# Attention from last tile to first, with WO work, QKV weights and the last x statistics in other slots (sliding dilated attention beside a ReLU feed-forward block, one core)

## The chip, the cores and the metric

The kernel runs on one core of a Trainium2 chip. The metric is the device time of one execution in microseconds (us). Five engines work side by side, each through its own instruction stream in order: TensorE (PE, matmuls; PEld is its weight load), VectorE (DVE), ScalarE (ACT), GpSimd (POOL) and SyncE (SP). SP issues most of the DMA transfers; POOL issues the transfers that add results to the output.

## The reference

`x` has 2048 tokens of 576 features, `wqkv` is 576 x 1728, `wo` 576 x 576, `w1` 576 x 4608, `w2` 4608 x 576, all float32.

```python
xn = _layernorm(x)                              # eps 1e-5, no gain, no bias
qkv = xn @ wqkv                                 # 32 heads of Dh = 18
idx = pos[:, None] - np.arange(8)[None, :] * 2  # W = 8 keys: this token and 7 before it, in steps of 2
logits = einsum("bhsd,bhswd->bhsw", q, kg) * Dh ** -0.5   # idx < 0 masked with -1e9
o = einsum("bhsw,bhswd->bhsd", softmax(logits), vg)
out = x + o.reshape(B, S, D) @ wo + maximum(xn @ w1, 0) @ w2
```

## The kernel before

**Two phases.** The step between keys is 2, so even and odd tokens never meet in the attention. The kernel therefore runs in two phases, `ph` 0 (even tokens) and 1 (odd). Each phase has 1024 tokens in eight tiles `i` of 128. Partition p holds the tokens 16p to 16p + 15 of the sequence, so the tiles of a phase are eight consecutive tokens of each partition. The key window of tile i, `window(k, i)`, is rows i to i + 7 of a block of 15 rows: rows 0 to 6 are the *halo*, a copy of the last seven key rows of the partition before (`halos`, four DMAs `att<-att`, L533), and rows 7 to 14 are the partition's own tiles. Value rows are laid out in the same way.

**Precision.** All products are made of float32 values split into a high and a low part: `two` copies the high part on ACT (L172) and subtracts for the low part on DVE (L176) or POOL (L174). Every weight goes through it before PE reads it.

**The feed-forward block** gives PE most of its work. The first six blocks of 128 hidden features per phase run in 24 *slots* (`BASE` 0 and 1000; `h_mm`, `h_two`, `o_mm`, `o_two`). The other 30 run in Strassen-like *groups* `g` of eight steps (`prologue` for group 0, then `group`), in pairs, whose `w1` blocks are loaded by `sw_load` (L895, L900), mixed on POOL (`sw_mix`) and split (`sw_prep`). `w2` blocks are loaded by L207. Matmuls on the two halves of the array, into different banks, run in pairs (L163; L142 for paired lists).

**QKV and attention.** The 32 heads are four units `u` of eight. QKV of unit 0 is computed in slots, of units 1 to 3 in groups 5, 11 and 17. After a unit's QKV its halos are copied, and `attention` puts its DVE work as a list of items into the queue `bg`: a multiply and a sum per tile for the logits (L563, L566), a mask on POOL (L569) after one of the sums, softmax, then a multiply and adds per tile for the values, and at the end a transpose and eight writes to DRAM (`o_out`, L618, L622). `run_bg(margin)` takes items off that queue while a planned DVE time stays within `margin` of a planned PE time; the plan (`t["pe"]`, `t["dve"]`) is made when the program is built. Buffers `pr` are used by turns, one at a time.

**WO.** When the last unit is written out, WO weights (`wo_load`, L257, L260) are split (`wo_split`, on ACT and DVE) and the attention rows come back (`ot_in`). `ot_plan` lists this work with delays, in us of the planned PE time, to the entry that it depends on: ("wl", 6 + ...) is that long after the WO loads. `wo_block(ph, r)` multiplies four tiles' rows by WO; `evict` copies PSUM to an `ev` tile (L711) and POOL adds it to the output. The blocks of phase 0 run in `seam`, between the phases, and in the first slots of phase 1, those of phase 1 in `epilogue`.

**x of phase 1** passes in phase 0 through `xq_load` (L404), `stats` (L303 to L307), `xq_norm` (L409), `turn` (L382) and `blocks_out` (L391), in the buffers of the attention tile that are free then.

**Order.** The kernel's order is written out by hand: each engine gets its instructions in the order of emission. `at(n, f)` emits f in slot n between the two halves of PE work (hidden features, then outputs), `late(n, f)` after the second. `on(ph, g, i, "T" or "O", f)` emits f in step i of group g, after the first or the second part of the step. A DMA's buffer and data dependences become semaphore waits of the instruction that needs them.

Of the kernel before, what the change touches and what calls it, by code (L numbers as in the profile page):

```python
# [19 lines left out]
P = 128  # L20
# [50 lines left out]
def tile_body(ctx: ExitStack, tc: tile.TileContext, x, wqkv, wo, w1, w2, out):  # L71
# [416 lines left out]
    def qkv_half(ph, u, tb, second, new):  # L488

        a = att(ph).rearrange("p (r c) -> p r c", c=UD)  # L490
        q0, v0 = Q_ROW[u % 2], V_ROW[u % 2]
        if tb == 0 and not second:
            assert len(bg) <= 26, (ph, u, len(bg))
            QO[ph, u] = a[:, q0 : q0 + NI]
            KK[ph, u] = a[:, K_ROW : K_ROW + W - 1 + NI]
            VV[ph, u] = a[:, v0 : v0 + W - 1 + NI]
        wq = WQ[ph, u]
        xt = XT[ph, tb]

        def run(h, terms):  # L500
            return [
                (PQ[h], xt[:, a, h * P : (h + 1) * P], wq[:, b, :], not second and j == 0, second and j == len(terms) - 1, 3 * UD)
                for j, (a, b) in enumerate(terms)
            ]

        if not second:
            if new:
                z = ps_o.tile([P, 2, 512], F32, name="po")
            for h in range(2):
                if new:  # L510
                    PQ[h] = z[:, h, 0 : 3 * UD]
                else:
                    PQ[h] = ps_m.tile([P, 3 * UD], F32, name="pm")
            PQ[2] = mm_rows((run(0, LOWER_MORE), run(1, UPPER_MORE)))
            return
        mm_rows((run(1, LOWER), run(0, UPPER)), PQ[2])
        for h in range(2):
            j, pq = 2 * tb + h, PQ.pop(h)
            step = K_ROW + W - 1 - q0
            nc.scalar.activation(  # L520
                a[:, q0 + j : q0 + j + 2 * step + 1 : step, :], pq.rearrange("p (s c) -> p s c", s=3), AF.Copy
            )
# [19 lines left out]
    def attention(ph, u):  # L542
# [15 lines left out]
        def qk_mul(i):  # L558
            if i % 2 == 0:
                both = prp.tile([P, 2, W, UD], F32, name="pr")  # L560
                pr[i], pr[i + 1] = both[:, 0], both[:, 1]
            q = qo[:, i, None, :].to_broadcast([P, W, UD])
            nc.vector.tensor_tensor(pr[i], q, window(k, i), op=ALU.mult)  # L563

        def qk_sum(i):
            nc.vector.tensor_reduce(lg[:, i], pr.pop(i).rearrange(heads, d=Dh), axis=AX.X, op=ALU.add)  # L566
            if i == NI - 2:
# [63 lines left out]
        for i in range(0, NI, 2):  # L631
            for f in (qk_mul, qk_sum):
                for j in (i, i + 1):
# [404 lines left out]
    def plan_strassen(ph):  # L1038
# [20 lines left out]
        for u in range(1, NU):  # L1059
# [9 lines left out]
            on(ph, g + 2, 2, "O", attention, ph, u)  # L1069
# [22 lines left out]
    def ot_plan(ph):  # L1092
# [4 lines left out]
        for kt in range(2, KT + 1):  # L1097
            z.append((("ws", kt), wo_split, (ph, kt), None, (("wl", 6 + 1.4 * (kt - 2)),)))
        for r in range(4):
            z.append((("in", r), ot_in, (ph, r), free if r == 3 else done, ((("in", r - 1), 5.0),) if r else (("wl", 5.0),)))  # L1100
# [33 lines left out]
    def prologue(ph, n0):  # L1134
# [24 lines left out]
        run_bg(1.0)  # L1159
# [75 lines left out]
    def wo_block(ph, r, parts=(0, 1, 2, 3)):  # L1235
        ot_go(ph, r)
        for k in parts:
            wo_half(ph, r, k % 2, k > 1)

# [104 lines left out]

    todo_late = {}
# [6 lines left out]
    for ph in range(NPH):  # L1352
# [15 lines left out]
        if ph == 0:  # L1368
# [4 lines left out]
            for i in range(NI):  # L1373
# [3 lines left out]
                late(n + 1 + odd, do)  # L1377
                if i < 6:
                    late(n + 2 + odd, xq_norm, i)
                    late(n + 2 + odd, turn, xq(i), 1, i)  # L1380
                    at(n + 4, blocks_out, xq(i), 1, i)
                else:
                    on(0, 0, 2 + 3 * odd, "O", xq_norm, i)
                    on(0, 0, 2 + 3 * odd, "O", turn, xq(i), 1, i)
                    on(0, 0, 7 + odd, "O", blocks_out, xq(i), 1, i)
                at(13 + i, nc.sync.dma_start, o_v[1, i], x_v[1, i])
        else:
# [3 lines left out]
            for r in range(1, NTB):  # L1391
                at(b + 3 * r, wo_block, 0, r)
            at(b + 10, wq_load, ph, 0)
# [5 lines left out]
        late(b + UNIT0[ph] + NI + 1, attention, ph, 0)  # L1399
# [118 lines left out]
    for ph in range(NPH):  # L1518
        b = BASE[ph]
        for n in range(b + (FIRST if ph == 0 else 0), b + NOLD - 2):  # L1520
            g = n - n % 2 + LAG
            if n < ROW0:
# [12 lines left out]
            run_bg(margin(n))  # L1535
# [31 lines left out]
```

## Time and profile before

| | us |
|---|---|
| median of 3 runs | 1171.43 |
| their range | 1170.77 to 1171.69 |
| the profiled execution | 1176.77 |
| its span in the trace | 1175.0 |
| PE busy in it | 1125.7 (96%) |
| DVE busy | 816.7 (70%) |
| ACT busy | 562.2 (48%) |
| POOL busy | 472.7 (40%) |

The profile shows one execution. The busy time of an engine is the time in which it has an instruction under way. A row of the timeline gives start, duration, engine, line and operation, the tiles (out<-in), and in square brackets how long the engine had stood idle before and what ended the wait. A row of the waits view gives the engine, tile and line that waited, what it waited for, the total in us, how often, and the longest. The granted clock is the share of full TensorE speed that the chip allowed; over the whole execution it is 0.984. Line numbers are those of the kernel before; in the changed kernel lines after L630 stand 3 lower, those of the end some more.

### The profile page before, as it was taken

Reading aid. Unit: us, or ns where it says so; the run is one execution under the profiler, and the core shown is the slowest. Engines: PE = TensorE matmul, PEld = TensorE weight load, DVE = VectorE, ACT = ScalarE, POOL = GpSimd, SP = SyncE. Lnnn points to the kernel's source line nnn. Section 1 sums busy time; section 2 is a strip of 40 time slices with the busy share of each in tenths; the row PEclk is TensorE's granted clock in tenths of the full one; section 3 lists DMA queues with packets and bytes.
Section 4 is the critical chain, followed back from the end, with each engine's and each line's share of the span. In section 5 each row is a group of like instructions: output and inputs, shape, how many; then the busy total and the mean of one; then the engine's idle time right before and its main releaser. Section 6 shows DMA issues by size and latency. Waiting matters only on the chain.

```text
span 1175.0 us, 38355 instructions
## 1 busy us (share of the span) xinstructions
PE 1125.7 (96%) x16410; PEld 1103.4 (94%) x16410; DVE 816.7 (70%) x1249; ACT 562.2 (48%) x1316; POOL 472.7 (40%) x514
## 2 busy tenths in 40 slices
PE   8999899999999999999997999999999999999996
PEld 8998899999999999998997999999999999999895
DVE  7675788698798788874315438877896886888431
ACT  4443463454355455556534235635644634555540
POOL 2323452353354355553323135434524523555331
PEclk9999899999999999999999999999999999999898
DMA  7479795786697598899947157858858957888984
GB/s 217 156 170 197 139 196 91 142 173 118 141 184 129 98 185 140 156 184 281 189 63 157 24 106 169 157 86 174 173 95 160 204 92 164 143 155 155 215 131 111
DMA packets 159810, 176.82 MB, mean 150 GB/s; under 512 B 36232, under 2 KB 107144, under 8 KB 159608
## 3 DMA queue, kind: packets, MB, share of 16 engines
q0 software_dynamic: 44352, 81.45, 47.5%
q1 hardware_dynamic: 114604, 92.03, 26.8%
q8 instruction: 129, 2.11, 0.7%
q10 hardware_dynamic: 684, 0.88, 0.2%
q14 instruction: 41, 0.34, 0.1%
HBM read 74.07 MB, written 95.70 MB: 144 GB/s over the span
## 4 chain that ended last, share of the span: by engine, by line
PE 73%; DMA 12%; DVE 6%; issue 3%; ACT 3%; SPq 2%; POOL 1%; DVEq 0%; ACTq 0%; POOLq 0%
PE po L163 23%; PE po L142 19%; PE ph L163 12%; PE pm L163 10%; PE pm L142 5%; DMA st<-in_w 4%; DMA out<-ev 3%; PE ph L142 3%; DVE ar L176 2%; DMA att<-od 1%; DMA att<-att 1%; ACT ev L711 1%; DMA xS<-od 1%; DMA od<-pr 1%; DVE ar L757 1%
## 5 line engine op out<-in xcount | busy, mean ns | idle before, releaser
L163 PE MATMUL po<-ar 64*128 64x320 f32 (+1 forms) x5760 | 475.6, 292 | 7.0 <-DVE ar L176 6.3
L163 PEld LDWEIGHTS po<-ar 64*128 64x128 f32 x5760 | 414.9, 186 | 11.3 <-DVE ar L176 9.0
L724 POOL DMA_DIRECT2D out<-ev x256 | 226.6, 1026 | 399.3 <-ACT ev L711 373.0
L163 PE MATMUL ph<-xT,ar 64*128 64x256 f32 x2520 | 328.7, 279 | 15.6 <-ACT pm L975 7.5
L163 PEld LDWEIGHTS ph<-xT,ar 64*128 64x128 f32 x2520 | 291.8, 187 | 21.9 <-ACT pm L975 12.3
L711 ACT ACTIVATE ev<-po 128x512 f32<-128x512 f32 (+1 forms) x268 | 172.8, 650 | 218.2 <-PE po L163 110.4
L163 PE MATMUL pm<-xS,ar 64*128 64x256 f32 x2160 | 267.9, 279 | 1.8 <-ACT u L979 0.7
L163 PEld LDWEIGHTS pm<-xS,ar 64*128 64x128 f32 x2160 | 242.3, 187 | 3.7 <-DVE ar L757 1.1
L176 DVE TENSOR_TENSOR ar<-st,ar 128x256 fp32r<-128x256 f32 (+3 forms) x232 | 146.1, 641 | 64.2 <-ACT ar L172 54.3
L172 ACT ACTIVATE ar<-st 128x256 fp32r<-128x256 f32 (+3 forms) x304 | 147.9, 500 | 21.5 <-DMA st<-in_w 16.2
L174 POOL TENSOR_TENSOR ar<-st,ar 128x256 fp32r<-128x256 f32 (+1 forms) x72 | 94.3, 1323 | 158.6 <-ACT ar L172 156.7
L907 POOL TENSOR_TENSOR st<-st 128x256 f32<-128x256 f32 x120 | 135.9, 1145 | 12.1 <-DMA st<-in_w 7.8
L142 PE MATMUL po<-wq,xT 64*128 64x432 f32 x1296 | 136.4, 353 | 0.0
L142 PEld LDWEIGHTS po<-wq,xT 64*128 64x128 f32 x1296 | 123.6, 184 | 1.5
L163 PE MATMUL ph<-xS,ar 64*128 64x256 f32 x720 | 103.2, 276 | 1.0 <-ACT ph L975 0.8
L563 DVE TENSOR_TENSOR pr<-att 128x1152 f32<-128x1152 f32 x64 | 89.3, 1399 | 18.4 <-DMA att<-att 18.2
L598 DVE TENSOR_TENSOR pr<-att 128x1152 f32<-128x1152 f32 x64 | 89.9, 1423 | 12.2 <-ACT att L520 11.9
L163 PEld LDWEIGHTS ph<-xS,ar 64*128 64x128 f32 x720 | 94.0, 184 | 2.6 <-ACT ph L975 2.0
L566 DVE TENSOR_REDUCE att<-pr 128x64 f32<-128x1152 f32 x64 | 84.9, 1338 | 0.0
L142 PE MATMUL po<-ar 64*128 64x256 f32 (+1 forms) x984 | 73.1, 293 | 2.7 <-ACT ev L711 2.7
L757 DVE SCALAR_TENSOR_TENSOR ar<-u,ar 128x256 fp32r<-128x256 f32 x60 | 31.7, 528 | 63.2 <-ACT ar L753 63.1
L605 DVE TENSOR_TENSOR pr<-pr 128x1152 f32<-128x1152 f32 x64 | 71.5, 1117 | 1.4
(120 smaller groups left out, 1356.4 us busy)
## 6 DMA issues: line engine op xcount, KB each, us to landing
out<-ev POOLq DMA_DIRECT2D x268, 288.0 KB, 6.2
st<-in_w SPq DMA_DIRECT2D x72, 288.0 KB
st<-in_w SPq DMA_DIRECT2D x120, 128.0 KB
att<-att SPq DMA_DIRECT2D x16, 441.0 KB
att<-in_wqkv SPq DMA_DIRECT2D x28, 216.0 KB
od<-pr SPq DMA_DIRECT2D x32, 128.0 KB
att<-in_x SPq DMA_DIRECT2D x14, 288.0 KB
st<-in_w SPq DMA_DIRECT2D x60, 64.0 KB
```

Of the source, the lines that this page charges most:

```text
L142: ins = nc.tensor.matmul(o, l[z], r[z], start=start, stop=stop)
L163: b.ins = nc.tensor.matmul(b.ap, l[part], r[part], start=start, stop=stop, skip_group_check=skip)
L172: nc.scalar.activation(hi, src, AF.Copy)
L174: nc.gpsimd.tensor_tensor(lo, src, f32(hi), op=ALU.subtract)
L176: nc.vector.tensor_tensor(lo, src, f32(hi), op=ALU.subtract)
L563: nc.vector.tensor_tensor(pr[i], q, window(k, i), op=ALU.mult)
L566: nc.vector.tensor_reduce(lg[:, i], pr.pop(i).rearrange(heads, d=Dh), axis=AX.X, op=ALU.add)
L598: nc.vector.tensor_tensor(pr[i].rearrange(heads, d=Dh), e, window(v, i).rearrange(heads, d=Dh), op=ALU.mult)
L605: nc.vector.tensor_tensor(o, z[:, :, 0:n], z[:, :, n : 2 * n], op=ALU.add)
L711: nc.scalar.activation(acc[:, :, cols], z[:, :, 0 : cols.stop - cols.start], AF.Copy)
L724: ADDED[ph, 2 * tb + k] = nc.gpsimd.dma_start(o_v[ph, 2 * tb + k], acc[:, k, :], accum_op=ALU.add)
L907: nc.gpsimd.tensor_tensor(stg(o), stg(a), stg(b), op=op)
```

## The change

Six things are changed in the order of emission; no instruction is added or removed.

1. `attention`: the logits are computed for tile 7, then 6, then 5 and 4 and so on down to 0; the mask on POOL follows the sum of tile 0 instead of tile 6, and the pair of tiles sharing a `pr` buffer is opened by the odd one. At unit changes `attention` is emitted at step 3 of its group instead of step 2, and for unit 0 one slot later. The queue may hold 30 items instead of 26 when the next unit's QKV begins.
2. The statistics of x tiles 6 and 7 of phase 1 go from slots to steps 1 and 5 of group 0, their norm, turn and `blocks_out` to group 1; for tiles 0 to 5 `blocks_out` goes from `at` to `late` of the same slot, so behind the next loads of x.
3. `ot_plan`: the splits of WO wait 8 + 2.0 (kt - 2) us behind the loads instead of 6 + 1.4 (kt - 2), and the first attention rows 6 us instead of 5.
4. In phase 1, WO block 1 of phase 0 stays in slot 3 but is emitted first in it; block 2 (slot 6) too, and block 3 comes with it (slot 9 before), evicted into a tile of the `pr` pool.
5. The load of the QKV weights of phase 1, unit 0, goes from slot 10 to slot 8.
6. `run_bg` has a margin of 0.3 instead of 1.0 in the prologue, and 1.4 less in one slot.

```diff
--- before.py
+++ after.py
@@ -490,7 +490,7 @@
         a = att(ph).rearrange("p (r c) -> p r c", c=UD)
         q0, v0 = Q_ROW[u % 2], V_ROW[u % 2]
         if tb == 0 and not second:
-            assert len(bg) <= 26, (ph, u, len(bg))
+            assert len(bg) <= 30, (ph, u, len(bg))
             QO[ph, u] = a[:, q0 : q0 + NI]
             KK[ph, u] = a[:, K_ROW : K_ROW + W - 1 + NI]
             VV[ph, u] = a[:, v0 : v0 + W - 1 + NI]
@@ -556,15 +556,15 @@
             return z[:, :, None, :].to_broadcast([P, NI, W, HG])
 
         def qk_mul(i):
-            if i % 2 == 0:
+            if i % 2:
                 both = prp.tile([P, 2, W, UD], F32, name="pr")
-                pr[i], pr[i + 1] = both[:, 0], both[:, 1]
+                pr[i], pr[i - 1] = both[:, 0], both[:, 1]
             q = qo[:, i, None, :].to_broadcast([P, W, UD])
             nc.vector.tensor_tensor(pr[i], q, window(k, i), op=ALU.mult)
 
         def qk_sum(i):
             nc.vector.tensor_reduce(lg[:, i], pr.pop(i).rearrange(heads, d=Dh), axis=AX.X, op=ALU.add)
-            if i == NI - 2:
+            if i == 0:
                 z = lg[0:1, 0 : NI - 1]
                 nc.gpsimd.affine_select(
                     out=z, in_=z, pattern=[[1, NI - 1], [1, W], [0, HG]], compare_op=ALU.is_ge,
@@ -628,9 +628,12 @@
 
         n, big = NI * W * HG, W * UD
         t["dve"] = max(t["dve"], t["pe"] - 1.5)
-        for i in range(0, NI, 2):
+        for j in (NI - 1, NI - 2):
             for f in (qk_mul, qk_sum):
-                for j in (i, i + 1):
+                bg.append((big, f, (j,)))
+        for i in range(NI - 3, 0, -2):
+            for f in (qk_mul, qk_sum):
+                for j in (i, i - 1):
                     bg.append((big, f, (j,)))
         for f in (sm_max, sm_sub, sm_exp, sm_sum, sm_rcp, sm_div):
             bg.append((0 if f is sm_exp else n + 520 if f in (sm_max, sm_sum) else n + 70, f, ()))
@@ -1066,7 +1069,7 @@
                 ins[ph, a, i].append((qkv_half, (ph, u, tb, False, True)))
                 ins[ph, a, i + 1].append((qkv_half, (ph, u, tb, True, True)))
             on(ph, g + 2, 1, "T", halos, ph, u)
-            on(ph, g + 2, 2, "O", attention, ph, u)
+            on(ph, g + 2, 3, "O", attention, ph, u)
         g = QKV_G[NU - 1] + 2
         on(ph, g, 1, "O", wo_first, ph)
         on(ph, g + 2, 3, "O", wo_split, ph, 0)
@@ -1095,9 +1098,9 @@
         free = lambda: done() and ("xs", ph) in hold
         z.append(("wl", wo_rest, (ph,), lambda: ph in ready, ()))
         for kt in range(2, KT + 1):
-            z.append((("ws", kt), wo_split, (ph, kt), None, (("wl", 6 + 1.4 * (kt - 2)),)))
+            z.append((("ws", kt), wo_split, (ph, kt), None, (("wl", 8 + 2.0 * (kt - 2)),)))
         for r in range(4):
-            z.append((("in", r), ot_in, (ph, r), free if r == 3 else done, ((("in", r - 1), 5.0),) if r else (("wl", 5.0),)))
+            z.append((("in", r), ot_in, (ph, r), free if r == 3 else done, ((("in", r - 1), 5.0),) if r else (("wl", 6.0),)))
             for h in range(2):
                 z.append((("split", r, h), ot_split, (ph, r, h), None, ((("in", r), 9.0 if ph or r == 0 else 22.0),)))
 
@@ -1156,7 +1159,7 @@
             fire(ph, g, i, "O")
         rows(M(ph, g, 6, last=True), M(ph, g, 2, last=True))
         seed(ph, g, "r", "q")
-        run_bg(1.0)
+        run_bg(0.3)
         rows(R(ph, g, 0, 0), R(ph, g, 1, 1))
         c_parts(ph, g, 0, 0, bank(ph, g, "a"))
         for i in (5, 6):
@@ -1237,6 +1240,10 @@
         for k in parts:
             wo_half(ph, r, k % 2, k > 1)
 
+    def wo_third():
+        EV[0, 3, "wo"] = prp.tile([P, 2, D], F32, name="pr"), []
+        wo_block(0, 3)
+
     def tail_end(ph, more):
         g = NG - 1
         tail = tail_lists(ph, g)
@@ -1341,6 +1348,11 @@
 
     def at(n, f, *a):
         todo.setdefault(n, []).append((f, a))
+
+    todo_first = {}
+
+    def first(n, f, *a):
+        todo_first.setdefault(n, []).append((f, a))
 
     todo_late = {}
 
@@ -1374,29 +1386,31 @@
                 n, odd = 9 + 4 * (i // 2), i % 2
                 at(n, xq_load, i)
                 do = lambda i=i: stats(1, i, xt=xq(i)[:, 0, :])
-                late(n + 1 + odd, do)
                 if i < 6:
+                    late(n + 1 + odd, do)
                     late(n + 2 + odd, xq_norm, i)
                     late(n + 2 + odd, turn, xq(i), 1, i)
-                    at(n + 4, blocks_out, xq(i), 1, i)
+                    late(n + 4, blocks_out, xq(i), 1, i)
                 else:
-                    on(0, 0, 2 + 3 * odd, "O", xq_norm, i)
-                    on(0, 0, 2 + 3 * odd, "O", turn, xq(i), 1, i)
-                    on(0, 0, 7 + odd, "O", blocks_out, xq(i), 1, i)
+                    on(0, 0, 1 + 4 * odd, "O", do)
+                    on(0, 1, 2 + 3 * odd, "O", xq_norm, i)
+                    on(0, 1, 2 + 3 * odd, "O", turn, xq(i), 1, i)
+                    on(0, 1, 5 + 3 * odd, "O", blocks_out, xq(i), 1, i)
                 at(13 + i, nc.sync.dma_start, o_v[1, i], x_v[1, i])
         else:
             for k in range(4):
                 late(b + (0, 1, 3, 4)[k], xt_parts, 1, 4 + k, 0)
                 late(b + (0, 1, 3, 4)[k], xt_parts, 1, 4 + k, 1)
-            for r in range(1, NTB):
-                at(b + 3 * r, wo_block, 0, r)
-            at(b + 10, wq_load, ph, 0)
+            first(b + 3, wo_block, 0, 1)
+            first(b + 6, wo_block, 0, 2)
+            first(b + 6, wo_third)
+            at(b + 8, wq_load, ph, 0)
             for kt in range(KT + 1):
                 late(b + 11 + kt // 3, wq_split, ph, 0, kt, kt % 2 == 1)
         late(b + (9, 13)[ph], zero_row, ph, K_ROW)
         late(b + (12, 14)[ph], zero_row, ph, V_ROW[0])
         at(b + UNIT0[ph] + NI, halos, ph, 0)
-        late(b + UNIT0[ph] + NI + 1, attention, ph, 0)
+        late(b + UNIT0[ph] + NI + 2, attention, ph, 0)
         late(b + 9, low_twin, ph, 0)
         late(b + 12, low_twin, ph, 2)
         for n in range(TS_SLOT[0], TS_SLOT[0] + 4):
@@ -1519,6 +1533,8 @@
         b = BASE[ph]
         for n in range(b + (FIRST if ph == 0 else 0), b + NOLD - 2):
             g = n - n % 2 + LAG
+            for f, a in todo_first.pop(n, []):
+                f(*a)
             if n < ROW0:
                 h_mm(n + LAG)
             else:
@@ -1532,7 +1548,7 @@
             for f, a in todo_late.pop(n, []):
                 f(*a)
             ot_go(0)
-            run_bg(margin(n))
+            run_bg(margin(n) - (1.4 if n == b + NOLD - 4 else 0.0))
         prologue(ph, b + NOLD - 2)
         for g in range(1, NG):
             group(ph, g)
```

## The prediction

> **What bounds the kernel now.** I read the page first, then the windows view at places where the granted clock drops, then the waits grouped by engine and line, and last the timeline around each long wait of TensorE. From the page:
>
> ```profile
> span 1175.0 us, 38355 instructions
> PE 1125.7 (96%) x16410; PEld 1103.4 (94%) x16410; DVE 816.7 (70%) x1249; ACT 562.2 (48%) x1316; POOL 472.7 (40%) x514
> ...
> PEclk9999899999999999999999999999999999999898
> ...
> PE 73%; DMA 12%; DVE 6%; issue 3%; ACT 3%; SPq 2%; POOL 1%; DVEq 0%; ACTq 0%; POOLq 0%
> ```
>
> TensorE (PE) is the bound, busy 96% of the span; no matmul is added or removed by the change. So it can win only what is left over: 1175.0 − 1125.7 = 49.3 us without work, and the time that PE runs at a reduced clock. The windows view (start:end, length, busy time of PE, PEld, DVE, ACT, POOL, then granted clock, DMA share, GB/s) shows the second part:
>
> ```profile
> 117.70:124.50 6.80, 3.77 (x32) 3.48 (x33) 5.62 (x14) 0.61 (x2) 3.70 (x5) 0.50 0.68 107
> 226.90:230.40 3.50, 3.50 (x34) 3.50 (x34) 3.50 (x6) 2.01 (x6) 0.40 (x1) 0.51 0.71 191
> 418.10:421.50 3.40, 3.40 (x34) 3.40 (x32) 3.40 (x6) 1.93 (x5) 0.18 (x1) 0.50 1.05 314
> 530.70:534.10 3.40, 3.40 (x34) 3.40 (x32) 0.59 (x2) 1.72 (x5) 0.86 (x1) 0.50 1.12 258
> 643.40:650.20 6.80, 6.04 (x40) 5.75 (x42) 6.39 (x12) 3.79 (x9) 1.97 (x2) 0.50 0.19 54
> 1104.20:1111.00 6.80, 6.23 (x54) 6.24 (x56) 2.29 (x5) 4.24 (x10) 2.91 (x4) 0.50 1.12 272
> ```
>
> In each of these PE works at half the clock, so that half of its busy time there is lost: 1.9, 1.7, 1.7, 1.7, 3.0 and 3.1 us. Each one stands a few microseconds behind a stall of PE. So a stall of 1.6 us can cost 3.3 us in all. The waits view (total us, times, longest us) names two that the change aims at; the others stand with their part below:
>
> ```profile
> DVE pr L563 <- DMA att<-att: 18.2, 6, 3.9
> ...
> PE po L163 <- DVE ar L176: 6.3, 7, 1.6
> ```
>
> VectorE (DVE) and ScalarE (ACT) work in the order in which the code emits. Whatever stands behind a waiting instruction waits too, and L176 and L172 (the hi/lo splits of weights) are what PE needs next.
>
> **The last x statistics (tiles 6, 7).** The timeline:
>
> ```profile
> 103.18 9.96 SPq L391 DMA_DIRECT2D words<-att  x8
> 113.18 0.98 SPq L404 DMA_DIRECT2D att<-in_x  x2
> 114.27 7.35 SPq L895 DMA_DIRECT2D st<-in_w  x4
> ...
> 116.96 0.82 DVE L303 BATCH_NORM_STATS2 bst<-att 128x6 f32<-128x288 f32 x2 [4.75 <-DMA att<-in_x]
> ...
> 120.67 0.58 PE L163 MATMUL ph<-xT,ar 64*128 64x256 f32 x1 [4.79 <-DVE ar L176]
> ```
>
> The loads of x tiles 6 and 7 (L404) stand on SP behind eight turned-block writes (L391, 9.96 us), land at 116.96, and DVE stands in front of the first statistics for 4.75 us with two L176 behind it; PE waits 4.79 us. In the changed order the loads go first, at about 103.2, so landing 116.96 − 113.18 = 3.8 us later, the second some 3 us behind the first, so by 107 and 110; the statistics stand behind the two splits, and the norms and turns a group later (costed at nothing: only the next phase reads them; without the cover of PE's long group they would cost their own DVE time, about that of the two rows of statistics). The stall (4.8) and its half clock (1.9) go: 6.7 us. Next late are the pair-1 weights: the loads at L895 move behind the writes and start some 3 to 4 us later than 114.27; mixing and splitting them I work out as ready just when PE needs them, within 0 to 1.5 us. I take 6.0 (0 to 6.7). The lower bg margin in the prologue (0.3 for 1.0) and the longer list (30 for 26) add no instruction; multiplies shift by one step, behind splits; if that cover were gone, one multiply (1.92 in the row of 222.75 below, at most) would stand before a split.
>
> **Attention from last tile to first, one step later.** At each of the unit changes:
>
> ```profile
> 216.59 0.44 SPq L622 DMA_DIRECT2D od<-pr  x1
> 217.13 3.21 SPq L533 DMA_DIRECT2D att<-att  x4
> ...
> 222.75 1.92 DVE L563 TENSOR_TENSOR pr<-att 128x1152 f32<-128x1152 f32 x1 [3.94 <-DMA att<-att]
> 224.59 0.81 DVE L176 TENSOR_TENSOR ar<-st,ar 128x256 fp32r<-128x256 f32 x2
> ...
> 225.46 0.56 PE L163 MATMUL po<-ar 64*128 64x320 f32 x4 [1.62 <-DVE ar L176]
> ...
> 990.97 0.56 PE L163 MATMUL po<-ar 64*128 64x320 f32 x4 [1.47 <-DVE ar L176]
> ```
>
> The first multiply (L563, tile 0) needs the halo rows, copied by four DMAs issued from 217.13; it starts at 222.75, and the two splits behind it make PE wait. The two PE rows are the first and the last of five such places, and five of the seven waits in the group of 6.3 us stand there. Emitted a step later, three splits stand ahead of the first multiply and need nothing from the halos. And tile 7, now first, uses key rows 7 to 14 of its own partition, no halo. It still writes a buffer that the last write-out (L622, 216.59) reads, so it starts when that landed; the next, tile 6, waits for the halos at about 222.6, but nothing that PE needs soon is behind it. So the five stalls go: 6.3 less half a microsecond for two others, 5.8; the short waits that follow each of them (some 0.2, five times, 1.1), and two half clocks (226.90 and 418.10), 3.4. Sum 10.3.
>
> Against it stands the causal mask, which now follows the last sum directly ahead of the softmax's maximum:
>
> ```profile
> L569 POOL TENSOR_SCALAR_AFFINE_SELECT att<-att x8: 975/976/1374, 164.8 to 1029.6; 1x448 f32<-1x448 f32 x8
> ...
> 175.00:200.00 25.00, 25.00 (x330) 24.60 (x329) 23.04 (x30) 10.74 (x25) 7.35 (x8) 1.00 0.47 78
> ```
>
> Eight times up to 1 us of DVE, in stretches where DVE is busy 23.04 of 25 us. Between them stand other DVE instructions for PE, so I see DVE waits of 0.3 to 0.5 us. On PE that is between 0 and 8 × 0.5 = 4; together with the step lost per unit I set 3.0 us against the total for places where DVE, nearly full, hands over a split late.
>
> **WO splits later, phase 0.**
>
> ```profile
> 525.21 0.69 ACT L172 ACTIVATE wq<-att 128x576 fp32r<-128x576 f32 x1 [2.41 <-DMA att<-wo]
> ...
> 530.40 0.38 PE L163 MATMUL ph<-xT,ar 64*128 64x256 f32 x1 [1.81 <-ACT pm L975]
> ...
> 516.00:548.00 32.00, 29.49 (x446) 28.72 (x444) 13.37 (x27) 19.12 (x43) 13.26 (x15) 0.95 1.08 258
> ...
> 550.35 0.63 ACT L422 ACTIVATE xT<-xT 128x512 fp32r<-128x512 f32 x1 [3.19 <-DMA xT<-words]
> 552.22 0.38 PE L142 MATMUL ph<-xT,ar 64*128 64x256 f32 x1 [0.60 <-ACT xT L422]
> ```
>
> ACT waits 2.41 us for a WO piece with an eviction and other splits behind, and PE pays 1.8 and the half clock at 530.70, 1.7: 3.5. Two microseconds more of delay cover the wait. But this stretch is full: the DMA share is 1.08 over 32 us, and the next phase's xT lands at 550.35, where PE already waits 0.60. PE would come there 3.5 us sooner and wait 4.1, long enough for a half clock too. So the gain is handed back, at worst with 3 more: −0.5, between +3.5 and −3.
>
> **WO blocks and the first QKV weights, phase 1.**
>
> ```profile
> 591.05 1.21 PE L142 MATMUL po<-ar 64*128 64x320 f32 x14 [0.45 <-ACT ev L711]
> ...
> 625.22 1.50 PE L142 MATMUL po<-ar 64*128 64x320 f32 x18 [0.45 <-ACT ev L711]
> ...
> 624.36 2.58 SPq L229 DMA_DIRECT2D att<-in_wqkv  x4
> ...
> 630.06 0.86 SPq L207 DMA_DIRECT2D st<-in_w  x1
> ...
> 642.88 0.78 ACT L172 ACTIVATE ar<-st 128x256 fp32r<-128x256 f32 x2 [6.97 <-DMA st<-in_w]
> ...
> 644.16 1.09 PE L142 MATMUL pm<-wq,xT 64*128 64x432 f32 x4 [6.00 <-ACT wq L172]
> ```
>
> The weights of QKV go into the attention buffer, which is free once the last WO block has read it, so their loads start at 624.36; a w2 load issued behind them at 630.06 lands only 12.8 us later, ACT waits for it (6.97) with the QKV splits behind it, and PE waits 6.00. Blocks 2 and 3 now come together three slots earlier, and the loads two; the two PE rows are the stalls at blocks 1 and 3, six slots apart, so a slot is (625.22 − 591.05) / 6 = 5.7 us, and I estimate the loads at 624.36 − 2 × 5.7 = 613 on, done by 618. Then both the w2 load and the splits are in time: gain 6.0 + 3.0 = 9.0 (6 to 9). Block 3 evicts into a tile of the `pr` pool, which DVE's sums of x (L447) must then wait for; the write-out starts about 613, those sums are due about 619, and if it landed later DVE would stand there with no split behind it for some microseconds: nothing, at worst 1. The three blocks' own stalls of 0.45 (1.35 us) shrink by half: 0.7.
>
> **WO splits later, phase 1.**
>
> ```profile
> 1100.61 0.68 ACT L172 ACTIVATE wq<-att 128x576 fp32r<-128x576 f32 x1 [3.84 <-DMA att<-wo]
> ...
> 1101.86 0.38 PE L163 MATMUL ph<-xT,ar 64*128 64x256 f32 x1 [1.34 <-ACT ar L172]
> ...
> 1104.77 0.58 PE L163 MATMUL ph<-xT,ar 64*128 64x256 f32 x1 [0.78 <-ACT pm L975]
> ```
>
> The same wait, 3.84 us, without the next phase's loads: PE loses 1.34 + 0.78, and 3.1 to the clock, 5.2. With the split two steps later some 0.75 stays at the step of 1104.77: 4.5 (2.5 to 5.2). That the attention rows come in 1 us later (wl + 6 for 5) I cost at nothing, because the matmuls still to run cover it; uncovered it is that 1 us.
>
> **The clock.** Whether short stalls bring the half clock matters for 6.5 us of this. The row at 226.90 stands behind a stall of 1.62 us and that at 418.10 behind one of at most 1.6. [...]
>
> **Sum.** 6.0 + 10.3 − 3.0 − 0.5 + 9.0 + 0.7 + 4.5 = 27.0 us. The profiled execution took 1176.77 us, 5.3 more than the median of 1171.43; off the median, 1171.43 − 27.0 = 1144.4.
>
> **The rivals.** (1) *Transfers keep their pace.* PE comes sooner, but the weights don't: the pair-1 weights loaded behind the eight writes cost the first item (0 for 6.0), the seam costs 3 for 0.5, the last WO pieces leave 2.5 for 4.5. Gain 27 − 6 − 2.5 − 2 = 16.5: 1155. For it: DMA share 1.08 in the seam. Against: 0.47 to 0.7 in the attention stretches. Chance 0.21. (2) *The half clocks behind short stalls are not theirs* and stay (226.90, 418.10, 1104.20: 6.5): 20.5, 1151. [...] (3) *Slower: attention falls behind.* The mask wait (0.98 us) and the later start push a unit's chain back, and the multiplies that DVE then takes in a row (1.92 us in the row of 222.75) stand ahead of splits. One such split makes PE wait about 1.6 us and brings a half clock, 1.7: 3.3 a time, as at 225.46. It decides when a chain is late by more than the 2 us that DVE has spare in 25. With two such places in each of eight units, 16 × 3.3 = 53 against the 30 that the sum has without its discount; from ten of the sixteen on nothing is won, and with twelve the time is 1171.4 − 30 + 40 = 1181. For it: 23.04 of 25. Against: DVE gets back the waits of 18.2 us in L563. Chance 0.09 for over 1174. (4) That the order doesn't take effect can't be: the engines follow the emission, and the changed program has the splits ahead.
>
> **How the numbers follow.** My case (1136 to 1150) has 0.60, rival 1 0.21, rival 2 0.05, 1155 to 1169 by other mishaps 0.02, same 0.03, slower 0.09. A measurement of this kernel tells 0.2% apart, 2.3 us. Faster 0.88, same 0.03, slower 0.09. The range: below, all upper bounds without the discount (6.7 + 10.3 + 3.5 + 9.0 + 1.35 + 5.2 = 36) give 1135; above, rival 1 with 6 us more lost to late splits, 1161.
>
> **What would show it.** Right: the granted clock is 1.00 at each of the six places, except perhaps the seam; DVE's wait for `att<-in_x` in L303 loses its 4.75; L563 still waits for a DMA at unit changes, but PE doesn't wait for L176 there; the QKV weight loads of phase 1 start two slots earlier and L142 waits no 6 us. Wrong: a PE wait for the pair-1 splits behind the seam of group 0, one over 3 us for xT at the seam, or L563 and L598 ahead of long PE waits in the middle of units.

## The result and the profile after

The changed kernel takes 1159.37 us (median of 4 runs, 1154.73 to 1162.72) against 1171.56 us before (4 runs, 1170.77 to 1174.45). The ratio is 0.9889, with a 95% interval from 0.9845 to 0.9933. It is faster by 12 us, not by the 27.0 us forecast. The profiled execution of the changed kernel took 1161.88 us.

From its page (the same lines as before the change):

```profile
span 1160.1 us, 38364 instructions
...
PE 1117.5 (96%) x16410; PEld 1096.8 (95%) x16410; DVE 816.0 (70%) x1249; ACT 559.7 (48%) x1316; POOL 474.6 (41%) x514
...
PEclk9999999999999999999999999999999999999999
```

The page counts nine instructions more than before, none of them among those that the row of the engines counts. PE's busy time is down by 8.2 us though it does the same matmuls: of six half-clock windows three are left. The idle time of PE went from 49.3 to 42.6 us. The waits view of the changed kernel tells what stands in the place of the stalls that went:

```profile
ACT ev L714 <- DMA out<-ev: 66.2, 23, 5.2
...
PE ph L163 <- ACT ph L978: 15.3, 11, 2.5
...
ACT att L675 <- DMA att<-od: 7.2, 2, 3.7
...
PE ph L163 <- ACT pm L978: 3.8, 8, 0.8
...
DVE bst L303 <- DMA att<-in_x: 3.6, 1, 3.6
...
PE po L163 <- DVE ar L176: 0.2, 1, 0.2
```

and the same view of the kernel before has

```profile
ACT ev L711 <- DMA out<-ev: 42.0, 19, 3.6
...
DVE bst L303 <- DMA att<-in_x: 15.0, 4, 4.7
...
PE ph L163 <- ACT pm L975: 7.5, 14, 1.8
...
PE ph L163 <- ACT ph L975: 0.8, 2, 0.6
```

The eviction of a result from PSUM (L711 before, L714 after) waits longer for the write-out of an older result tile. PE waits for L978 (L975 before), a copy on ACT that seeds a PSUM bank, `ph` or `pm`: 15.3 and 3.8 us, 19.1 in all, against 0.8 and 7.5, 8.3 in all, before. Of the 15.3 us, 9.3 are five stalls behind an eviction that waits for a write-out (2.25, 2.38, 1.23, 1.97 and 1.45), and 4.7 are two stalls behind the split of the attention rows, L675 (2.19 and 2.54). Before, the evictions already waited 42.0 us for write-outs, and PE paid little for it. PE's wait for L176 in the units has gone from 6.3 us to 0.2. DVE's waits in the x statistics went from 15.0 to 3.6 us. ACT's wait for the attention rows (L675) is new; before, no row of the view had it.

**Where the time came from.** PE's matmuls have the same order in both traces, apart from three WO blocks, so the n-th matmul can be compared. The lead of the changed kernel grows and shrinks like this (times of the kernel before, one execution of each kernel; the shares were worked out from the starts of every hundredth matmul):

| stretch | lead won, us | forecast, us |
|---|---|---|
| to 207: last x statistics | 6.7 | 6.0 |
| 207 to 515 and 699 to 1090: attention | 1.5 − 2.3 = −0.8 | 10.3 − 3.0 |
| 515 to 575: seam, WO splits | 0.0 | −0.5 |
| 575 to 633: WO blocks | −0.2 | 0.7 |
| 633 to 699: first QKV weights | 7.8 | 9.0 |
| from 1090: WO splits | 1.3 | 4.5 |

The attention is the largest hole. The timeline of the changed kernel at the unit change that stood at 222 before:

```profile
214.23 1.77 POOL L727 DMA_DIRECT2D out<-ev  x2 [6.81 <-ACT ev L714]
...
225.17 0.60 ACT L714 ACTIVATE ev<-po 128x512 f32<-128x512 f32 x1 [5.04 <-DMA out<-ev]
...
226.80 0.37 ACT L978 ACTIVATE ph<-ph 128x256 f32<-128x256 f32 x1
...
227.22 0.39 PE L163 MATMUL ph<-xS,ar 64*128 64x256 f32 x1 [2.25 <-ACT ph L978]
```

and the kernel before at the same instructions:

```profile
220.91 1.77 POOL L724 DMA_DIRECT2D out<-ev  x2 [6.82 <-ACT ev L711]
...
232.50 0.60 ACT L711 ACTIVATE ev<-po 128x512 f32<-128x512 f32 x1 [1.84 <-PE po L163]
```

There are two result tiles (`evp`). ACT may fill one again when both halves of its write-out, issued on POOL, have landed. Before, 11.6 us passed between that issue and the eviction, and ACT came too late to notice: PE had stood 1.62 us for DVE's split and had run 3.5 us at half the clock. After, those are gone as forecast, ACT is ready 5.9 us after the issue, and the second half lands only at 225.1. So ACT stands 5.04 us, and PE 2.25 us. The old stall had covered the write-out.

At the last x statistics the loads, the splits and the statistics stand as forecast:

```profile
102.65 3.54 SPq L404 DMA_DIRECT2D att<-in_x  x2
106.25 8.00 SPq L391 DMA_DIRECT2D words<-att  x8
114.35 2.35 SPq L898 DMA_DIRECT2D st<-in_w  x4
...
113.59 0.69 DVE L176 TENSOR_TENSOR ar<-st,ar 128x512 fp32r<-128x512 f32 x1 [1.33 <-ACT ar L172]
114.20 0.81 DVE L303 BATCH_NORM_STATS2 bst<-att 128x6 f32<-128x288 f32 x2
```

The loads stand ahead of the eight writes, L176 ahead of the statistics, and these wait for nothing. The w1 loads of pair 1 (L898) start at 114.35; before (L895) it was 114.27, so that they are not the forecast 3 to 4 us later. At the end of phase 1 ACT waits again, but for something else:

```profile
1085.87 0.69 ACT L172 ACTIVATE wq<-att 128x576 fp32r<-128x576 f32 x1 [1.10 <-DMA att<-wo]
...
1095.80 0.74 ACT L675 ACTIVATE att<-att 128x640 fp32r<-128x640 f32 x1 [3.69 <-DMA att<-od]
...
1098.88 0.38 PE L163 MATMUL ph<-xS,ar 64*128 64x256 f32 x1 [2.54 <-ACT ph L978]
```

The WO piece costs 1.10 us in place of 3.84; the split of the first attention rows (L675), ten microseconds later, costs 3.69, and PE 2.54 behind it.

### The profile page after: what moved, and what is told of

Same layout as the page of the kernel before. It is cut to its first block, busy times and chain, and to the rows that moved or that the text cites. A ratio compares the mean times of both kernels' runs of the same rounds, so it can differ in the third digit from the quotient of the medians.

```text
span 1160.1 us, 38364 instructions
## 1 busy us (share of the span) xinstructions
PE 1117.5 (96%) x16410; PEld 1096.8 (95%) x16410; DVE 816.0 (70%) x1249; ACT 559.7 (48%) x1316; POOL 474.6 (41%) x514
## 4 chain that ended last, share of the span: by engine, by line
PE 67%; DMA 16%; DVE 5%; ACT 4%; issue 3%; SPq 2%; POOL 2%; ACTq 0%; DVEq 0%; POOLq 0%
PE po L163 20%; PE po L142 18%; PE ph L163 11%; PE pm L163 8%; DMA out<-ev 7%; PE pm L142 4%; PE ph L142 3%; DMA att<-od 2%; DMA st<-in_w 2%; ACT ev L714 1%; DVE ar L176 1%; POOL out L727 1%; PE ph L130 1%; PE po L130 1%; DMA xS<-out 1%
## 5 line engine op out<-in xcount | busy, mean ns | idle before, releaser
L163 PE MATMUL po<-ar 64*128 64x320 f32 (+1 forms) x5760 | 483.9, 291 | 1.6 <-ACT ev L714 1.0
L163 PEld LDWEIGHTS po<-ar 64*128 64x128 f32 x5760 | 424.4, 186 | 4.7 <-ACT ev L714 1.6
L714 ACT ACTIVATE ev<-po 128x512 f32<-128x512 f32 (+1 forms) x266 | 171.4, 650 | 216.6 <-PE po L163 90.3
L163 PE MATMUL pm<-xS,ar 64*128 64x256 f32 x2160 | 262.5, 276 | 1.6 <-ACT u L982 0.9
L163 PEld LDWEIGHTS pm<-xS,ar 64*128 64x128 f32 x2160 | 239.0, 184 | 3.1 <-ACT u L982 1.3
L176 DVE TENSOR_TENSOR ar<-st,ar 128x256 fp32r<-128x256 f32 (+3 forms) x232 | 146.9, 643 | 72.5 <-ACT ar L172 59.5
L174 POOL TENSOR_TENSOR ar<-st,ar 128x256 fp32r<-128x256 f32 (+1 forms) x72 | 97.2, 1354 | 170.4 <-ACT ar L172 167.2
L163 PE MATMUL ph<-xS,ar 64*128 64x256 f32 x720 | 106.4, 281 | 15.5 <-ACT ph L978 15.3
L163 PEld LDWEIGHTS ph<-xS,ar 64*128 64x128 f32 x720 | 95.9, 188 | 19.1 <-ACT ph L978 18.2
L563 DVE TENSOR_TENSOR pr<-att 128x1152 f32<-128x1152 f32 x64 | 86.6, 1355 | 0.3
```

Source lines behind the costliest of these rows:

```text
L163: b.ins = nc.tensor.matmul(b.ap, l[part], r[part], start=start, stop=stop, skip_group_check=skip)
L174: nc.gpsimd.tensor_tensor(lo, src, f32(hi), op=ALU.subtract)
L176: nc.vector.tensor_tensor(lo, src, f32(hi), op=ALU.subtract)
L714: nc.scalar.activation(acc[:, :, cols], z[:, :, 0 : cols.stop - cols.start], AF.Copy)
```

## The experiments

The edits are to the changed kernel, or to the kernel before where "alone" is said. Each was timed in 6 or 12 runs (the changed kernel in 4), beside the kernel before, whose median was 1171.76, 1171.51 and 1170.56 us in the three groups. The ratios, with their 95% intervals:

| kernel | median, us | ratio | interval |
|---|---|---|---|
| changed kernel | 1159.37 | 0.9889 | 0.9845 to 0.9933 |
| attention part undone | 1154.51 | 0.9862 | 0.9834 to 0.9890 |
| attention part alone | 1174.04 | 1.0007 | 0.9983 to 1.0031 |
| value halos later | 1160.26 | 0.9902 | 0.9875 to 0.9929 |
| attention rows split later | 1160.00 | 0.9897 | 0.9870 to 0.9924 |
| five half tiles | 1151.67 | 0.9841 | 0.9807 to 0.9876 |
| five half tiles, attention part undone | 1156.82 | 0.9874 | 0.9844 to 0.9904 |
| WO and rows split later | 1156.30 | 0.9881 | 0.9842 to 0.9920 |
| x statistics alone | 1163.10 | 0.9936 | 0.9913 to 0.9959 |
| WO blocks and QKV weights alone | 1168.73 | 0.9980 | 0.9956 to 1.0004 |
| WO splits alone | 1170.75 | 0.9999 | 0.9974 to 1.0024 |
| five half tiles, phase 1 later | 1148.20 | 0.9800 | 0.9765 to 0.9834 |
| attention part and five half tiles alone | 1159.21 | 0.9897 | 0.9861 to 0.9932 |

**Is the attention part worth anything?** First it was undone (the core of the edit is shown), and then done alone, by the same edit the other way on the kernel before.

```diff
-        for j in (NI - 1, NI - 2):
-            for f in (qk_mul, qk_sum):
-                bg.append((big, f, (j,)))
-        for i in range(NI - 3, 0, -2):
+        for i in range(0, NI, 2):
             for f in (qk_mul, qk_sum):
-                for j in (i, i - 1):
+                for j in (i, i + 1):
                     bg.append((big, f, (j,)))
...
-            on(ph, g + 2, 3, "O", attention, ph, u)
+            on(ph, g + 2, 2, "O", attention, ph, u)
...
-        late(b + UNIT0[ph] + NI + 2, attention, ph, 0)
+        late(b + UNIT0[ph] + NI + 1, attention, ph, 0)
```

> The changed kernel with the attention part alone undone: tiles first to last, mask after the sum of tile 6, emission at step 2 and one slot earlier. Theory of the write-out ring: the stalls that the new order takes away (10.3 us) come back as stalls of ScalarE, which waits for a write-out of an earlier result tile, so the part is worth about nothing: 1157 to 1162 us, with VectorE waiting again for the halo copies at unit changes and no PE wait of 2 us for L978 there. Rival, the prediction's step: the part is worth 7 us, so this kernel takes 1166 or more.

> The kernel before with the attention part alone. Theory of the ring: 1169 to 1173 us; at the unit changes PE waits some 2 us for L978 in place of 1.5 for L176. Rival, the prediction's step: 1164 us.

Undone it is 1154.51 us, a little faster than the changed kernel (the intervals overlap) and 2.5 us faster than the theory allowed; alone, 1174.04 us or 1.0007, 1 us above what the theory had. The waits view of the second, attention alone:

```profile
ACT ev L714 <- DMA out<-ev: 68.6, 25, 5.0
...
PE ph L163 <- ACT ph L978: 9.6, 9, 2.2
...
PE po L163 <- DVE ar L176: 0.2, 1, 0.2
```

The prediction's step falls: the part takes the stalls behind L176 away, 6.3 us to 0.2, and gains nothing.

**Is it the traffic of the halos?** The copy of the value halos, which only the second half of a unit's attention reads, was put behind the next w1 loads.

```diff
-        for z in KK[ph, u], VV[ph, u]:
-            for a, b in HALO:
-                nc.sync.dma_start(z[a + 1 : b + 1, 0 : W - 1, :], z[a:b, NI : NI + W - 1, :])
+        halo_rows(KK[ph, u])
+        if u == 0:
+            halo_rows(VV[ph, u])
+
+    def halo_rows(z):
+        for a, b in HALO:
+            nc.sync.dma_start(z[a + 1 : b + 1, 0 : W - 1, :], z[a:b, NI : NI + W - 1, :])
+
+    def v_halos(ph, u):
+        halo_rows(VV[ph, u])
...
             on(ph, g + 2, 3, "O", attention, ph, u)
+            on(ph, g + 3, 5, "O", v_halos, ph, u)
```

> The changed kernel with the value halos of units 1 to 3 copied a group later, behind the next w1 loads on SP. Theory: the write-out of a result tile lands 2 us later than before because halos and weight loads are in flight with it; with half of the halos gone it lands 2 to 2.5 us earlier, ScalarE's wait of 5 us falls below 3 and the PE stalls of 1.2 to 2.4 us at four unit changes go: 1149 to 1153 us. Rival: the halos have nothing to do with it (two result tiles are too few at any traffic, or the weight loads are the cause): 1157 to 1162, waits of 5 us stay.

1160.26: nothing won, and in the rival's range. The timeline shows that the stall moved:

```profile
222.80 0.60 ACT L721 ACTIVATE ev<-po 128x512 f32<-128x512 f32 x1 [2.82 <-DMA out<-ev]
...
249.48 0.60 ACT L721 ACTIVATE ev<-po 128x512 f32<-128x512 f32 x1 [4.19 <-DMA out<-ev]
...
251.99 0.39 PE L163 MATMUL ph<-xS,ar 64*128 64x256 f32 x1 [2.21 <-ACT ph L985]
```

At the first unit change the wait fell from 5.04 to 2.82 and PE lost nothing, as the theory had it. But 27 us later a wait of 4.19 stands where the changed kernel had less than 2, and PE pays 2.21. At the third unit change the wait is as long as before (5.1 for 5.17), and all waits for write-outs together are 70.9 us for 66.2. So here the traffic of the halos changed where the write-out is late, but not whether it is late somewhere.

**Is it the number of result tiles?** Five half tiles, used by turns, in place of two whole ones; the room comes from unused columns of the QKV weight tile, whose matmuls keep their mean duration (355 ns against 353). The last that a new tile has to wait for is then the first half of the tile before last, and not its second.

```diff
-    evp = pool("evp", 2)
+    evp = pool("evp", 1)
...
+    ring = evp.tile([P, 5, D], F32, name="ev")
+    def ev_pair():
+        n = count["ev"] = count.get("ev", -1) + 1
+        a = 2 * n % 5
+        return ring[:, 0:5:4, :] if a == 4 else ring[:, a : a + 2, :]
...
-WQ0, WQS = 60, 448
+WQ0, WQS = 0, 432
```

> The changed kernel with two and a half result tiles in place of two: five half tiles used by turns (room for it comes from the unused columns in the QKV weight tile). An eviction then waits only for the first of the two write-outs of the tile before last, which lands 1.3 to 3.5 us before the second. Theory of the ring: the waits of ScalarE for write-outs (66 us in all in the changed kernel) fall to a third, and the PE stalls for L978 at unit changes and in the middle of units go, with their half clocks: 1148 to 1153 us. Rival (the ring is only where a slower DMA shows, and the stalls come back at the next thing that DMA brings): 1156 to 1161.

> The same five half tiles, with the attention part undone. Theory of the ring: with the ring out of the way the attention part is worth what its stalls cost, here 4 us (0.9, 0.3, 0.9, 0.9 and 1.5 without it), so this kernel is 2 to 6 us slower than the one with it. Rival: the attention part costs time by itself (the mask, the later start), and this kernel is the faster of the two, 1150 to 1153.

> The kernel before with the attention part and the five half tiles, nothing else. Theory of the ring: the attention part, worth nothing alone (1174 against 1172), is worth 4 to 7 us once the ring doesn't hold ScalarE: 1164 to 1168. Rival: the five half tiles gain by some other way, or the attention part costs time itself: 1169 to 1173.

1151.67 with the attention part and 1156.82 without; alone on the kernel before, 1159.21. The waits view of the changed kernel with five half tiles:

```profile
PE ph L163 <- ACT pm L985: 6.1, 10, 2.3
...
ACT ev L721 <- DMA out<-ev: 5.4, 2, 5.2
PE ph L163 <- ACT ph L985: 4.8, 3, 2.4
```

and of the one with five half tiles and the attention part undone:

```profile
ACT ev L718 <- DMA out<-ev: 14.5, 6, 3.4
...
PE po L163 <- DVE ar L176: 6.3, 7, 1.5
```

and of the attention part and the five half tiles alone, where the attention part by itself had 68.6 us:

```profile
ACT ev L721 <- DMA out<-ev: 14.9, 8, 3.5
...
PE ph L163 <- ACT pm L985: 3.8, 9, 0.8
```

In the changed kernel the waits for write-outs fall from 66.2 to 5.4 us, and PE's for the seeding copy from 19.1 to 10.9, both kinds of bank taken together; one stall of 2.39 us behind a write-out is left, at the last unit change. Without the attention part the waits for write-outs fall too, from 49.5 to 14.5, but there PE stands behind L176 as before, and the half tile gives nothing (0.9874 against 0.9862). The clearest pair is attention alone, 1.0007, against attention and five half tiles alone, 0.9897: intervals far apart, 13 us. So the theory of the ring holds: neither of the two gained anything where it was tried without the other. The half tiles by themselves on the kernel before were not tried.

What the two are worth together is not settled. On the kernel before it is 12 us, more than the 4 to 7 that were expected; on the changed kernel with the attention part undone it is 2.5 (0.9841 against 0.9862, the intervals overlap). A part of the difference may lie in the half clocks. PE stands behind L176 in the units for 6.3 us in the trace before, 5.2 with the attention part undone and 6.3 with the five half tiles beside that. In five traces with the old order of the attention (the kernel before, the part undone, and the x statistics, the QKV weights and the WO splits alone) a half-clock window follows such a stall twice, not at all, once, not at all and twice. The sum of the prediction took the two of one execution, 3.4 us; the mean is one, 1.7.

**The WO pieces.** First the rows were split later, then the WO pieces too, and the change's own part was run alone.

```diff
-((("in", r), 9.0 if ph or r == 0 else 22.0),)
+((("in", r), 12.5 if ph or r == 0 else 22.0),)
```

That is the edit of the first kernel; the second has it too, and

```diff
-(("wl", 8 + 2.0 * (kt - 2)),)
+(("wl", 11 + 2.0 * (kt - 2)),)
```

> The changed kernel with the split of the first attention rows 12.5 us behind their load in place of 9. Theory: at both phase ends ScalarE waits 3.5 to 3.7 us for these rows in place of the WO pieces, and PE 2.2 and 2.5 us behind it, once or twice with a half clock of 1.5 to 3 us; 3.5 us later the rows are there. At the end of phase 1 4 us are won, at the seam 0 to 2, since xT sets the time there: 1153 to 1156. Rival: the write-outs of results are the next wait at the same place, so that PE stalls on: 1158 to 1160.

> The changed kernel with the WO splits 11 + 2 (kt - 2) us behind the loads in place of 8 + 2 (kt - 2), and the first attention rows split 12.5 us behind theirs. Theory: the WO pieces take 5.6 to 9 us from issue to landing, so that 8 us of planned time are too short in some executions; with 11 neither they nor the rows are waited for at the end of phase 1, and PE's stalls of 2.5 to 4 us there go, with a half clock: 1154 to 1157. Rival: what is late moves on to the next, the write-outs or the rows, 1158 to 1161.

> The kernel before with the longer delays of the WO splits alone. The prediction's step: 4.5 us at the end of phase 1 and nothing at the seam: 1167. Theory after the runs so far: the WO pieces and the attention rows land up to 9 and 12 us after their issue, so that ScalarE waits at the same place for the one or the other: 0 to 2 us won, 1169 to 1172.

1160.00, where the rival's time came, 1156.30 and 1170.75, as the theory had them. The first shows, at the end of phase 1,

```profile
1085.28 0.68 ACT L172 ACTIVATE wq<-att 128x576 fp32r<-128x576 f32 x1 [4.96 <-DMA att<-wo]
...
1087.89 0.58 PE L163 MATMUL ph<-xT,ar 64*128 64x256 f32 x1 [4.04 <-ACT pm L978]
```

the second, at the seam,

```profile
532.34 0.78 ACT L172 ACTIVATE ar<-st 128x256 fp32r<-128x256 f32 x2 [4.29 <-DMA st<-in_w]
...
536.23 0.58 PE L163 MATMUL ph<-xT,ar 64*128 64x256 f32 x1 [4.55 <-ACT pm L978]
```

and the change's part alone, on the kernel before,

```profile
1095.63 0.68 ACT L172 ACTIVATE wq<-att 128x576 fp32r<-128x576 f32 x1 [4.02 <-DMA att<-wo]
...
1097.95 0.58 PE L163 MATMUL ph<-xT,ar 64*128 64x256 f32 x1 [2.81 <-ACT pm L975]
```

So the WO piece is waited for at its new place too: in all seven traces with this delay ACT waits for it at the end of phase 1, 1.1 to 5.0 us, against 3.8 to 5.8 in the five with the old one. 8 us of planned time are not enough. With 11 us that wait is gone from both ends; at the seam a w2 block takes its place, at the end of phase 1 a stall of 1.43 us is left. Whether the second is faster than the changed kernel the intervals don't tell.

**The parts that worked, alone.** Only the lines of the change that belong to each were put into the kernel before; the x statistics have the lower margin of the prologue with them.

> The kernel before with the part on the last x statistics alone. The prediction's step: the stall of 4.8 us and its half clock go, 6 to 6.7 us: 1165 us. Rival: the weights of pair 1, loaded behind the eight writes, take it back: 1168 to 1171.

> The kernel before with the WO blocks of phase 1 and the load of the QKV weights alone moved. The prediction's step: the stall of 6.0 us and its half clock of 3.0 go, with 0.7 at the blocks: 9.7 us, 1162. What the two traces before and after show between these places is 7.6 us: 1164. Rival (the stall of 6 us was a chance of one execution): 1168 to 1170.

The x statistics alone win 7.5 us (0.9936): the step holds. The stall that they take away was 4.79 us in the trace before, and in the four other traces with this part unchanged it was about 4 to 6.11 us, each time with 6.8 us or more at half clock, so it is there in every execution seen. The QKV weights win 2.3 us (0.9980, the interval reaches 1.0004), not 9.7. Why, two executions show in which this part is unchanged; the first is the x statistics alone, the second the WO splits alone:

```profile
629.74 1.43 PE L142 MATMUL pm<-wq,xT 64*128 64x432 f32 x12 [1.97 <-ACT wq L172]
```

```profile
640.31 2.01 PE L142 MATMUL pm<-wq,xT 64*128 64x432 f32 x18 [2.20 <-ACT wq L172]
```

The stall that was 6.00 us in the profiled execution before is about 2 us here, and also in the two traces of attention alone (2.24 and 2.03, the latter with five half tiles), and none of the four has a half clock behind it. The trace of before showed an unlucky execution: it took 1176.77 us where the median is 1171. In the trace of the kernel with the part alone a new stall of 1.57 us, behind a DVE split, stands near the same place.

**The best version**: five half tiles, and in phase 1 alone the longer delays.

```diff
-(("wl", 8 + 2.0 * (kt - 2)),)
+(("wl", (11 if ph else 8) + 2.0 * (kt - 2)),)
...
-((("in", r), 9.0 if ph or r == 0 else 22.0),)
+((("in", r), 12.5 if ph else 9.0 if r == 0 else 22.0),)
```

> The changed kernel with five half tiles for results, and in phase 1 alone the WO splits 11 us and the first attention rows 12.5 us behind their loads. Theory: with the ring out of the way the write-outs don't take the place of the WO pieces, so the stalls of 2.3 and 0.4 us at the end of phase 1 and a half clock go: 2 to 4 us faster than with the five half tiles alone, 1147 to 1150. Rival: 1151 to 1153.

1148.20 us, 0.9800 (0.9765 to 0.9834): the interval lies below that of the changed kernel. Against the five half tiles alone it is 3 us less, as expected, though those intervals overlap.

## Why the prediction was wrong, and where it was right

- **What bounds the kernel, the half clocks**: right. PE does the same work; half-clock windows fell from six to three, and PE's busy time by 8.2 us. The sign of a granted clock of 1.00 at each of the six places came out at three of them: at the third unit change (417), the seam (530) and the end of phase 1 (1100) one is left. And not each one stands behind its stall: those at 117.70 and 643.40 begin within it.
- **The last x statistics, 6.0**: right; 6.7 in the traces and 7.5 alone. PE did not wait for the weights of pair 1, the feared cost; their loads started no later than before, because loads and writes only changed places.
- **Attention, 10.3 less 3.0**: the failed step. Its first half is right: in the changed kernel PE no longer waits behind L176 at unit changes, and L563 doesn't wait for the halos either, though the prediction expected it to. What is wrong is the step from there to a gain, "So the five stalls go", for nothing else was looked at that had to be in time 3.4 us sooner (1.62 and half of 3.50). The write-outs of results had to, and the waits view of before named them with 42.0 us in 19 waits; the prediction leaves that row out. At four of the six unit changes in groups PE now pays 1.2 to 2.4 us for it, and elsewhere 1.45. The discount of 3.0 was for the wrong cause, the mask and a full DVE: DVE waited once for the mask, 1.1 us. Of the 10.3 itself, 3.4 were the two half clocks of one execution. With five half tiles beside it there is a gain: 12 us for both together on the kernel before, and on the changed kernel 4 us for the part (0.9841 against 0.9874, where the intervals overlap).
- **Rival 1, "transfers keep their pace"** named the kind of cause, and its 1155 is the nearest of the single times to what was measured (the time itself lies in the 1155 to 1169 "by other mishaps", which had a chance of 0.02), but it had the transfers at the wrong places: pair-1 weights, seam and WO pieces, not the write-outs in the units. **Rival 3** foresaw PE losing time in the units, to DVE; the loss came through ACT. **Rival 2** fell, though not by the changed kernel, where other stalls came to its three places. With five half tiles PE works without a stall from 215 to 235 and from 410 to 422, round the first and the third unit change, and there, as everywhere in that execution before its last 10 us, it has no half clock.
- **The QKV weights, 9.0**: the term was mis-sized. The mechanism is right (no wait of 6 us, loads at 605 in place of 624), but 6.0 + 3.0 is what one execution lost. Alone it measured 2.3. The profiled execution was 5.3 us above the median; the sum took that difference off as a constant and did not ask which stalls it was made of.
- **WO splits of phase 1, 4.5**: failed. Alone, the part gives 0.1. The step "two microseconds more of delay cover the wait" took the landing from one execution, and at the end of phase 1 it set 2.0 us against a wait of 3.84; by the ends of ACT's waits there, the pieces are in place 5.6 to 9 us after their issue. And the attention rows behind them, whose later start was costed at nothing "because the matmuls still to run cover it", are late next: ACT waits 3.52 and 3.69 us for them and PE 2.19 and 2.54.
- **The seam, −0.5**: right in size (0.0 between these two executions), though by way of L675 (3.52 us of wait, PE 2.19) and not of xT, for which PE waits 0.69 us, about as before.
- **WO blocks, 0.7**: −0.2.

Put together, the parts alone give 7.5 − 0.8 + 2.3 + 0.1 = 9.1 us, the whole 12 to 13; forecast were 27.0, of which the attention (8 missing), the QKV weights (7) and the WO splits (4) were not there.

## What to carry to other kernels

When a stall on the bounding engine is taken away, everything that ran during it has that much less time: look at every buffer that goes round (here two result tiles and the landing of their write-outs) and ask when its next use comes, not only at what stood behind the stalled instruction. A stall seen in one execution is worth its mean over executions; if the profiled time lies above the median, some of its stalls are not in the median. A fixed delay ahead of a transfer has to cover its slowest landing, and then that of the next transfer in line.

## What the runs showed of the hardware

The second half of a write-out issued by POOL landed after 8.0 us in the trace before and after 10.25 us in the one after, at the same instructions, with a second w2 load issued 1.3 us behind the write-out in place of 4.5, the next w1 load 2.6 us in place of 5.3, and the next write-out 5.8 us in place of 9.1. Which of these made the difference was not tried by itself; the halos alone, copied later, shortened this wait (2.82 us for 5.04) and lengthened another (4.19 us for less than 2).

The half clock does not follow from the length of a stall alone. In the changed kernel a stall of 2.25 us has none behind it, in the windows view from 224.00, while in the kernel before one of 1.47 us has one (the row at 418.10). The first two rows are the changed kernel's; the second shows the half clock behind the stall of 2.38 us at 416:

```profile
224.00:231.00 7.00, 4.75 (x76) 4.52 (x76) 4.83 (x7) 4.24 (x11) 3.42 (x3) 1.00 0.37 66
...
414.00:424.00 10.00, 7.62 (x98) 7.61 (x99) 8.25 (x10) 5.71 (x14) 4.70 (x4) 0.83 0.70 131
...
222.79:226.20 3.41, 2.19 (x33) 1.95 (x29) 0.10 (x1) 1.03 (x3) 0.00 (x0) 1.00 0.84 138
226.20:229.61 3.41, 2.39 (x41) 2.39 (x42) 3.35 (x5) 2.69 (x7) 2.03 (x2) 1.00 0.17 44
```

and, in the kernel before, the stretch ahead of the half clock at 418.10:

```profile
414.69:418.10 3.41, 1.71 (x21) 1.19 (x19) 3.41 (x5) 1.02 (x3) 1.26 (x1) 1.00 0.97 171
```

Where a stall falls counts beside its length. But for the one at the very end (8.0 and 7.5 us), each half clock lasts 6.83 or 3.41 us in the trace before (three of each) and 3.41 us in the one after (all three); in the windows of nine further runs it is 3.4, 6.8 or, once, 10.2 us. In the trace before they start at 117.71, 226.94, 418.08, 530.72, 643.36 and 1104.16, in the one after at 417.36, 530.00 and 1100.03, in each trace whole multiples of 3.41 us apart; the last three rows are stretches of 3.41 us cut at such multiples. The stall of 2.25 us falls across two of them, in which PE idles 1.22 and 1.02 us. The stall of 1.47 us, with a wait of 0.23 behind it, falls into one, which has 1.70 us idle. With both traces cut that way, 666 stretches are at full clock. Of the 654 with less than 1.6 us of PE idle time none has a half clock in the stretch behind it, of the five with 1.6 to 1.9 us four have one, and all seven with 2.0 us or more. So in these two traces what follows a stall of 1.5 to 2.5 us depends on where it falls as well.
